# Hash-bucket attention and a max-out feed-forward on one core: operands transposed by DMA, exponentials as the stationary operand, feed-forward interleaved half-batch by half-batch

## The chip, the cores and the metric

One core of a Trainium2 chip. The metric is the device time of one execution in microseconds. Runs of one kernel on one chip differ by 0.3 to 5% here; a run more than 1.5% above the fastest of its kernel counts as slow, and verdicts use the others ("fast runs"). Engines: TensorE (PE; its weight loads, PEld, overlap its matmuls), VectorE (DVE), ScalarE (ACT), GpSimd (POOL), SyncE (SP), which issues DMAs.

## The reference

Attention over 4 batches x 8 heads x 768 tokens x 64 dimensions. A query sees only the keys whose 6-bit hash (signs of a projection) equals its own; a query without such a key gets the mean of v. The result, as 3072 tokens x 512, goes through a feed-forward with three input weights.

```python
q_bucket = sum(((q @ proj) > 0) * 2**arange(6)); k_bucket likewise
scores = where(q_bucket == k_bucket, 0.125 * q @ k.T, -1e9)
attn = softmax(scores) @ v                      # per head, 768 x 768
x = attn as (3072, 512)
h = max(x @ w1, x @ w2, x @ w3)                 # 512 -> 768
out = h @ w_out                                 # 768 -> 512
```

The six bits are appended to the 64 dimensions of q and k as large numbers, so one matmul with 70 rows gives score plus a bucket term, and Exp with a bias turns unequal buckets into zeros.

## The kernel before

A pair of heads at a time: fp32 q and k are transposed on TensorE, copied out of PSUM, hashed by fp32 matmuls; then scores, Exp in two pieces, and attention-value (AV) matmuls with v stationary and 768 exponentials moving. The denominators land on one row and go through DRAM to become a factor on all rows. After all 16 pairs comes the feed-forward.

```python
def prep(pi):                                    # [cut: loads]
    for natt, dsts in ((qnat, qa), (knat, ka)):
        mp = misc_ps.tile([P, S], FP32, tag="m1")
        for c in range(NCH):
            nc.tensor.transpose(mp[:, c*P:(c+1)*P], natt[:, c, :], iden[:])      # L107
        nc.vector.tensor_copy(dsts[0][0:D, :], mp[0:D, :])                       # L108
        nc.vector.tensor_copy(dsts[1][0:D, :], mp[D:2*D, :])
    # [cut] bps <- P2, qa / ka in fp32 (L114, L116); signs written into rows 64..69
def body(pi):
    for hd, von in ((0, voneA), (1, voneB)):
        for c in range(NCH):
            # [cut] two score matmuls, 512 + 256 columns (L147)
            nc.scalar.activation(AT[:, 0:512], sc[:, 0:512], ActFn.Exp, ...)     # L150
            nc.scalar.activation(AT[:, 512:768], sc[:, 512:768], ActFn.Exp, ...) # L151
            nc.tensor.matmul(av[0:65, 0:512], von[:, c, :], AT[:, 0:512], ...)   # L154
            nc.tensor.matmul(av[0:65, 512:768], von[:, c, :], AT[:, 512:768], ...)
        # [cut] svp <- v column sums (L158); row 64 through DRAM; normalise into xT
prep(0)
for pi in range(NPAIR):
    if pi + 1 < NPAIR: prep(pi + 1)
    body(pi)
# [cut] then the feed-forward over 6 chunks of 512 tokens (L221, L232)
```

The softmax here doesn't subtract the row's maximum and nothing guards it: scores larger than these inputs give would overflow.

Of the kernel before, what the change touches and what calls it, by code (L numbers as in the profile page):

```python
# [11 lines left out]
BF16 = mybir.dt.bfloat16  # L12
# [5 lines left out]
def kernel(  # L18
# [17 lines left out]
    NT = B * S  # L36
    DM = H * D
    DF = moe_w1.shape[1]
    NPAIR = (B * H) // 2
    HPAIR = H // 2  # L40
    NB2 = D + NBITS

    SCALE = 0.125
    EXP_BIAS = -SCALE * 256.0 * NBITS

    konst = ctx.enter_context(tc.tile_pool(name="konst", bufs=1))
    wpool = ctx.enter_context(tc.tile_pool(name="wpool", bufs=1))
    xpool = ctx.enter_context(tc.tile_pool(name="xpool", bufs=1))

    iden = konst.tile([P, P], FP32, name="iden")  # L50
    make_identity(nc, iden[:])
    P2 = konst.tile([P, NBITS], FP32, name="P2")
    nc.sync.dma_start(P2[0:D, :], proj[:, :])
    ones_row = konst.tile([P, D], FP16, name="ones_row")
    nc.vector.memset(ones_row[:], 1.0)
    bias_t = konst.tile([P, 1], FP32, name="bias_t")
    nc.vector.memset(bias_t[:], EXP_BIAS)

    w1_sb = wpool.tile([P, DM // P, DF], FP16, name="w1_sb")
    w2_sb = wpool.tile([P, DM // P, DF], FP16, name="w2_sb")  # L60
    w3_sb = wpool.tile([P, DM // P, DF], FP16, name="w3_sb")
    for w_sb, w_ap in ((w1_sb, moe_w1), (w2_sb, moe_w2), (w3_sb, moe_w3)):
        nc.gpsimd.dma_start(w_sb[:], w_ap.rearrange("(c p) f -> p c f", p=P))
    wout_sb = wpool.tile([P, DF // P, DM], FP16, name="wout_sb")
    nc.gpsimd.dma_start(wout_sb[:], moe_w_out.rearrange("(c p) m -> p c m", p=P))

    xT = [xpool.tile([P, NT], FP16, name=f"xT{j}", tag=f"xT{j}") for j in range(DM // P)]

    NVBUF = 3
    vone_tiles = [konst.tile([P, NCH, D + 1], FP16, name=f"vone{i}", tag=f"vone{i}")  # L70
                  for i in range(2 * NVBUF)]
    for t in vone_tiles:
        nc.vector.memset(t[:, :, D : D + 1], 1.0)

    att_ctx = ExitStack()
    nat = att_ctx.enter_context(tc.tile_pool(name="nat", bufs=4))
    ptile = att_ctx.enter_context(tc.tile_pool(name="ptile", bufs=3))
    atp = att_ctx.enter_context(tc.tile_pool(name="atp", bufs=10))
    small = att_ctx.enter_context(tc.tile_pool(name="small", bufs=4))
    drp = att_ctx.enter_context(tc.tile_pool(name="drp", bufs=4, space=bass.MemoryType.DRAM))  # L80
    sc_ps = att_ctx.enter_context(tc.tile_pool(name="sc_ps", bufs=2, space=bass.MemoryType.PSUM))
    misc_ps = att_ctx.enter_context(tc.tile_pool(name="misc_ps", bufs=1, space=bass.MemoryType.PSUM))
    av_ps = att_ctx.enter_context(tc.tile_pool(name="av_ps", bufs=1, space=bass.MemoryType.PSUM))

    pair_state = {}

    def prep(pi):
        b = pi // HPAIR
        jj = pi % HPAIR
        hA, hB = 2 * jj, 2 * jj + 1  # L90
        qnat = nat.tile([P, NCH, 2 * D], FP32, tag="qnat")
        knat = nat.tile([P, NCH, 2 * D], FP32, tag="knat")
        nc.sync.dma_start(qnat[:, :, 0:D], q[b, hA].rearrange("(c p) d -> p c d", p=P))
        nc.sync.dma_start(qnat[:, :, D : 2 * D], q[b, hB].rearrange("(c p) d -> p c d", p=P))
        nc.sync.dma_start(knat[:, :, 0:D], k[b, hA].rearrange("(c p) d -> p c d", p=P))
        nc.sync.dma_start(knat[:, :, D : 2 * D], k[b, hB].rearrange("(c p) d -> p c d", p=P))
        voneA = vone_tiles[(pi % NVBUF)]
        voneB = vone_tiles[NVBUF + (pi % NVBUF)]
        nc.gpsimd.dma_start(voneA[:, :, 0:D], v[b, hA].rearrange("(c p) d -> p c d", p=P))
        nc.gpsimd.dma_start(voneB[:, :, 0:D], v[b, hB].rearrange("(c p) d -> p c d", p=P))  # L100

        qa = [ptile.tile([NB2, S], FP32, tag="qaA", name="qaA"), ptile.tile([NB2, S], FP32, tag="qaB", name="qaB")]
        ka = [ptile.tile([NB2, S], FP32, tag="kaA", name="kaA"), ptile.tile([NB2, S], FP32, tag="kaB", name="kaB")]
        for natt, dsts in ((qnat, qa), (knat, ka)):
            mp = misc_ps.tile([P, S], FP32, tag="m1")
            for c in range(NCH):
                nc.tensor.transpose(mp[:, c * P : (c + 1) * P], natt[:, c, :], iden[:])  # L107
            nc.vector.tensor_copy(dsts[0][0:D, :], mp[0:D, :])  # L108
            nc.vector.tensor_copy(dsts[1][0:D, :], mp[D : 2 * D, :])

        for src, qside in ((qa, True), (ka, False)):
            bps = misc_ps.tile([P, S], FP32, tag="m1")
            for col0, nn in ((0, 512), (512, 256)):
                nc.tensor.matmul(bps[0:NBITS, col0 : col0 + nn], P2[0:D, :],  # L114
                                 src[0][0:D, col0 : col0 + nn], start=True, stop=True)
                nc.tensor.matmul(bps[64 : 64 + NBITS, col0 : col0 + nn], P2[0:D, :],  # L116
                                 src[1][0:D, col0 : col0 + nn], start=True, stop=True)
            for hd, base in ((0, 0), (1, 64)):
                o = src[hd][D : D + NBITS, 0:S]
                i_ = bps[base : base + NBITS, 0:S]  # L120
                if qside:
                    nc.vector.tensor_scalar(out=o, in0=i_, scalar1=0.0, scalar2=0.5,  # L122
                                            op0=AluOp.is_gt, op1=AluOp.subtract)
                else:
                    nc.vector.tensor_scalar(out=o, in0=i_, scalar1=0.0, scalar2=1024.0,  # L125
                                            op0=AluOp.is_gt, op1=AluOp.mult)
                    nc.vector.tensor_scalar(out=o, in0=o, scalar1=512.0, scalar2=None,
                                            op0=AluOp.subtract)
        pair_state[pi] = (qa, ka, voneA, voneB)

    def body(pi):
        b = pi // HPAIR
        jj = pi % HPAIR
        xt_tile = xT[jj]
        xcol = b * S
        qa, ka, voneA, voneB = pair_state.pop(pi)
        qab = [t.bitcast(BF16)[:, 1::2] for t in qa]
        kab = [t.bitcast(BF16)[:, 1::2] for t in ka]

        avs_h = []  # L140
        for hd, von in ((0, voneA), (1, voneB)):
            av = av_ps.tile([65, 1024], FP32, tag="av")
            for c in range(NCH):
                AT = atp.tile([P, S], FP16, tag="AT")
                sc = sc_ps.tile([P, S], FP32, tag="sc")
                for col0, nn in ((0, 512), (512, 256)):
                    nc.tensor.matmul(sc[:, col0 : col0 + nn],  # L147
                                     kab[hd][0:NB2, c * P : (c + 1) * P],
                                     qab[hd][0:NB2, col0 : col0 + nn], start=True, stop=True)
                nc.scalar.activation(AT[:, 0:512], sc[:, 0:512], ActFn.Exp, bias=bias_t[:], scale=SCALE)  # L150
                nc.scalar.activation(AT[:, 512:768], sc[:, 512:768], ActFn.Exp, bias=bias_t[:], scale=SCALE)  # L151
                st = c == 0
                sp = c == NCH - 1
                nc.tensor.matmul(av[0:65, 0:512], von[:, c, :], AT[:, 0:512], start=st, stop=sp)  # L154
                nc.tensor.matmul(av[0:65, 512:768], von[:, c, :], AT[:, 512:768], start=st, stop=sp)  # L155
            svp = sc_ps.tile([P, S], FP32, tag="sc")
            for c in range(NCH):
                nc.tensor.matmul(svp[0:D, 0:1], von[:, c, 0:D], ones_row[:, 0:1],  # L158
                                 start=(c == 0), stop=(c == NCH - 1))
            avs = small.tile([65, 776], FP32, tag="avs")  # L160
            nc.scalar.copy(avs[0:65, 0:768], av[0:65, 0:768])  # L161
            nc.vector.tensor_copy(avs[0:D, 768:769], svp[0:D, 0:1])  # L162
            avs_h.append(avs)

        for hd in (0, 1):
            avs = avs_h[hd]
            dlt = small.tile([65, S], FP16, tag="dlt")
            nc.vector.tensor_scalar(out=dlt[64:65, :], in0=avs[64:65, 0:768], scalar1=0.01,
                                    scalar2=None, op0=AluOp.is_lt)
            dra = drp.tile([S], FP32, tag="dra")  # L170
            drb_ = drp.tile([S], FP16, tag="drb_")
# [24 lines left out]
    for pi in range(NPAIR):  # L196
        if pi + 1 < NPAIR:
            prep(pi + 1)
        body(pi)
# [68 lines left out]
```

## Time and profile before

510.6 us, the median of 2 runs (506.13 and 515.07); the profiled run spans 517.3 us. By the rule above the slower of the two is a slow run, and so is the profiled one.

| stage of the span | us | what fills it |
|---|---|---|
| start | 0-25 | TensorE waits for q and k |
| attention | 25-386 | no engine full; TensorE at 0.68-0.83 of its clock |
| feed-forward | 386-517 | TensorE full, clock 1.0 |

The span in 40 slices of 12.9 us (kernel before), busy tenths, and the granted TensorE clock (the share of its full clock that TensorE was given) in tenths:

```profile
PE   0258888899879798989889788898989999999996
...
PEclk9999969757796877566676996757579999999999
```

The next lines are stretches of the same trace: busy time and count of each engine, then granted clock, DMA share and GB/s.

```profile
100.00:200.00 100.00, 85.75 (x398) 39.06 (x398) 67.83 (x110) 61.88 (x120) 37.91 (x65) 0.78 0.37 64
200.00:300.00 100.00, 88.63 (x376) 42.29 (x376) 64.19 (x104) 58.91 (x114) 35.29 (x62) 0.69 0.31 52
400.00:450.00 50.00, 49.02 (x228) 22.12 (x227) 20.12 (x29) 13.55 (x24) 0.25 (x1) 1.00 0.13 49
```

The attention stage has TensorE 86-89% busy at a reduced clock, DVE 64-68%, ACT about 60%: a chain rather than a full engine. The costliest groups there (the page's list: busy us and mean ns of one, then idle time before and what ended it):

```profile
L150 ACT ACTIVATE AT<-sc,bias_t 128x512 f16<-128x512 f32 x192 | 132.2, 689 | 140.5 <-PE sc L147 140.4
L151 ACT ACTIVATE AT<-sc,bias_t 128x256 f16<-128x256 f32 x192 | 90.9, 473 | 0.0
...
L114 PE MATMUL bps<-kaA,P_69 64*6 64x512 f32 (+1 forms) x64 | 35.2, 692 | 11.3 <-DVE qaB L122 11.3
L107 PE MATMUL mp<-iden,qnat 128*128 128x128 f32 x96 | 30.2, 394 | 16.7 <-DMA qnat<-in_q_dram 14.1
```

One line of the timeline (start, length, engine, line): six matmuls of one column, each with its own 64-column weight load. One takes 0.171 us, so (0.35 - 0.17) / 5 = 36 ns from start to start.

```profile
65.45 0.35 PE L158 MATMUL svp<-ones_row,vone_88 128*64 128x1 f16 x6
```

### The profile page before, as it was taken

How to read it: one execution, taken by the hardware profiler on the slowest of the kernel's cores; microseconds unless marked ns; L12 is line 12 of the kernel's file. 1: busy time of each engine (PE TensorE's matmuls, PEld its weight loads, DVE VectorE, ACT ScalarE, POOL GpSimd, SP SyncE). 2: the span in 40 equal slices, each digit the busy share in tenths (PEclk: the TensorE clock that was granted, in tenths of full speed). 3: DMA queues.
4: the chain of work that ended last, by engine and by line, in shares of the span. 5: the costliest groups of instructions: out<-in, count | busy, mean ns of one | idle time of the engine just before them, and what ended most of it. 6: DMA issues, size and time to landing. Idle time of an engine off the chain costs nothing.

```text
span 517.3 us, 5907 instructions
## 1 busy us (share of the span) xinstructions
PE 440.8 (85%) x1984; PEld 205.4 (40%) x1984; DVE 287.6 (56%) x464; ACT 253.4 (49%) x477; POOL 133.0 (26%) x234
## 2 busy tenths in 40 slices
PE   0258888899879798989889788898989999999996
PEld 0113433425334253534444344443444444444442
DVE  0145658756776667565575785766437353353442
ACT  0005857648575565555655676556682313323232
POOL 6000434423433334333333443323233000000000
PEclk9999969757796877566676996757579999999999
DMA  9994524415242533414141321201010202102012
GB/s 155 186 213 100 90 36 86 83 26 93 40 85 39 86 55 63 85 25 86 24 84 25 40 33 24 25 16 24 10 32 18 89 0 82 62 20 82 22 61 83
DMA packets 88367, 32.16 MB, mean 62 GB/s; under 512 B 80912, under 2 KB 84240, under 8 KB 88336
## 3 DMA queue, kind: packets, MB, share of 16 engines
q0 software_dynamic: 34624, 12.89, 17.7%
q1 hardware_dynamic: 53712, 18.88, 14.8%
q8 instruction: 16, 0.26, 0.2%
q14 instruction: 15, 0.12, 0.1%
HBM read 31.56 MB, written 6.49 MB: 74 GB/s over the span
## 4 chain that ended last, share of the span: by engine, by line
PE 58%; issue 12%; DVE 11%; DMA 9%; ACT 6%; POOL 3%; ACTq 0%; POOLq 0%; DVEq 0%
PE av L154 10%; PE sc L147 9%; PE bps L114 8%; PE pso L232 6%; PE mp L107 5%; ACT AT L150 5%; PE av L155 5%; DMA vone_87<-in_v_dram 4%; DVE avs L189 2%; DVE qaB L122 2%; DVE qaA L122 1%; ACT avs L161 1%; DMA dra<-avs 1%; PE svp L158 1%; DMA drb__335<-r_339 1%
## 5 line engine op out<-in xcount | busy, mean ns | idle before, releaser
L150 ACT ACTIVATE AT<-sc,bias_t 128x512 f16<-128x512 f32 x192 | 132.2, 689 | 140.5 <-PE sc L147 140.4
L151 ACT ACTIVATE AT<-sc,bias_t 128x256 f16<-128x256 f32 x192 | 90.9, 473 | 0.0
L147 PE MATMUL sc<-qaB,kaB 70*128 70x512 bf16 x192 | 67.8, 461 | 0.0
L221 PEld LDWEIGHTS <-w_sb 128*128 128x128 f16 x432 | 42.3, 98 | 51.0 <-issue 0.3
L147 PE MATMUL sc<-qaA,kaA 70*128 70x512 bf16 x192 | 55.0, 389 | 0.5 <-DVE avs L162 0.5
L114 PE MATMUL bps<-kaA,P_69 64*6 64x512 f32 (+1 forms) x64 | 35.2, 692 | 11.3 <-DVE qaB L122 11.3
L107 PE MATMUL mp<-iden,qnat 128*128 128x128 f32 x96 | 30.2, 394 | 16.7 <-DMA qnat<-in_q_dram 14.1
L161 ACT COPY avs<-av 65x768 f32<-65x768 f32 x32 | 25.4, 795 | 28.9 <-PE av L155 28.9
L116 PE MATMUL bps<-kaB,P_69 64*6 64x512 f32 (+1 forms) x64 | 35.4, 695 | 0.0
L147 PEld LDWEIGHTS <-kaB 70*128 70x128 bf16 x192 | 25.0, 131 | 25.0 <-issue 19.0
L189 DVE SCALAR_TENSOR_TENSOR avs<-dltb,avs 64x768 f32<-64x768 f16 x32 | 31.9, 997 | 0.4
L125 DVE TENSOR_SCALAR kaA<-bps 6x768 f32<-6x768 f32 x16 | 15.2, 949 | 26.8 <-PE bps L116 26.8
L147 PEld LDWEIGHTS <-kaA 70*128 70x128 bf16 x192 | 22.1, 115 | 19.6 <-issue 12.7
L108 DVE COPY qaA<-mp 64x768 f32<-64x768 f32 x16 | 15.1, 946 | 25.5 <-PE mp L107 25.5
L108 DVE COPY kaA<-mp 64x768 f32<-64x768 f32 x16 | 15.2, 950 | 25.0 <-PE mp L107 24.9
L107 PEld LDWEIGHTS mp<-iden,qnat 128*128 128x128 f32 x96 | 18.0, 204 | 27.5 <-issue 23.5
L114 PE MATMUL bps<-qaA,P_69 64*6 64x512 f32 (+1 forms) x64 | 25.2, 517 | 3.6 <-issue 2.1
L235 ACT COPY osb<-pso 128x512 f32<-128x512 f32 x24 | 14.1, 586 | 28.8 <-PE pso L232 28.8
L107 PE MATMUL mp<-iden,knat 128*128 128x128 f32 x96 | 18.8, 342 | 9.2 <-DMA knat<-in_k_dram 8.4
L116 PE MATMUL bps<-qaB,P_69 64*6 64x512 f32 (+1 forms) x64 | 25.2, 517 | 0.0
L122 DVE TENSOR_SCALAR qaA<-bps 6x768 f32<-6x768 f32 x16 | 15.2, 949 | 16.4 <-PE bps L116 16.3
L154 PE MATMUL av<-AT,vone_87 128*65 128x512 f16 x36 | 16.9, 468 | 7.7 <-ACT AT L150 7.0
(882 smaller groups left out, 841.4 us busy)
## 6 DMA issues: line engine op xcount, KB each, us to landing
qnat<-in_q_dram SPq DMA_DIRECT2D x32, 192.0 KB, 3.0
knat<-in_k_dram SPq DMA_DIRECT2D x32, 192.0 KB, 3.2
out_dram<-osb SPq DMA_DIRECT2D x24, 256.0 KB, 2.0
dltb<-ddl POOLq DMA_DIRECT2D x32, 96.0 KB, 2.6
w_sb<-in_moe_w_dram POOLq DMA_DIRECT2D x3, 768.0 KB, 11.3
wout_sb<-in_moe_w_out_dram POOLq DMA_DIRECT2D x1, 768.0 KB, 19.2
vone_87<-in_v_dram POOLq DMA_DIRECT2D x6, 96.0 KB, 3.2
vone_90<-in_v_dram POOLq DMA_DIRECT2D x6, 96.0 KB, 3.2
```

Source lines behind the costliest of these rows:

```text
L107: nc.tensor.transpose(mp[:, c * P : (c + 1) * P], natt[:, c, :], iden[:])
L114: nc.tensor.matmul(bps[0:NBITS, col0 : col0 + nn], P2[0:D, :], src[0][0:D, col0 : col0 + nn], start=True, stop=True)
L116: nc.tensor.matmul(bps[64 : 64 + NBITS, col0 : col0 + nn], P2[0:D, :], src[1][0:D, col0 : col0 + nn], start=True, stop=True)
L122: nc.vector.tensor_scalar(out=o, in0=i_, scalar1=0.0, scalar2=0.5, op0=AluOp.is_gt, op1=AluOp.subtract)
L147: nc.tensor.matmul(sc[:, col0 : col0 + nn], kab[hd][0:NB2, c * P : (c + 1) * P], qab[hd][0:NB2, col0 : col0 + nn], start=True, stop=True)
L150: nc.scalar.activation(AT[:, 0:512], sc[:, 0:512], ActFn.Exp, bias=bias_t[:], scale=SCALE)
L151: nc.scalar.activation(AT[:, 512:768], sc[:, 512:768], ActFn.Exp, bias=bias_t[:], scale=SCALE)
L154: nc.tensor.matmul(av[0:65, 0:512], von[:, c, :], AT[:, 0:512], start=st, stop=sp)
L161: nc.scalar.copy(avs[0:65, 0:768], av[0:65, 0:768])
L189: nc.vector.scalar_tensor_tensor(out=avs[0:D, 0:768], in0=dltb[:, :], scalar=avs[0:D, 768:769], in1=avs[0:D, 0:768], op0=AluOp.mult, op1=A ...
L221: nc.tensor.matmul(psx[:, :], w_sb[:, jc, fb * P : (fb + 1) * P], xT[jc][:, tcx * TOK : (tcx + 1) * TOK], start=(jc == 0), stop=(jc == NJC ...
L232: nc.tensor.matmul(pso[:, :], hts[fb][:, tb * P : (tb + 1) * P], wout_sb[:, fb, :], start=(fb == 0), stop=(fb == NFB - 1))
```

## The change

Intent: take the fp32 work and the PSUM copies off the attention stage, halve the AV columns, drop the DRAM round trips, and let the feed-forward fill TensorE while attention waits.

- q and k are **split** on DVE into an fp16 pair (value and remainder), side by side in 128 columns, and **transposed by DMA** (40 transposes of 384 KB). Hashes are fp16 matmuls on the pair, four column groups at once.
- **AV is turned round**: a 128x128 block of exponentials is stationary, 65 columns of v and ones move. The denominator is then a column, and normalising stays on the chip (DVE; POOL adds the mean of v where it is needed).
- The order is fixed by hand. A **step** is one score/Exp/AV unit (two key chunks, half the queries of one head); there are 192. A **half-batch** is 24 steps. When one is complete it is transposed by DMA into xT, and its 21 feed-forward groups are dealt out over later steps by a **credit** counter.

```diff
-            nc.tensor.transpose(mp[:, c * P : (c + 1) * P], natt[:, c, :], iden[:])
+            nc.vector.tensor_scalar(out=s[:, :, 0:D], in0=x32, scalar1=QS, ...)          # L121
+            nc.vector.scalar_tensor_tensor(out=s[:, :, D : 2 * D], in0=x32, scalar=QS,
+                                           in1=s[:, :, 0:D], ...)                        # L122
+            nc.sync.dma_start_transpose(t[:], s[:].rearrange("p a d -> p (a d)"))        # L125
 [cut: hashes, L133; score, L186, and one Exp of 768 columns, L190]
-            nc.tensor.matmul(av[0:65, 0:512], von[:, c, :], AT[:, 0:512], ...)
+                nc.tensor.matmul(av[:, o : o + D + 1], AT[:, i, c * P : (c + 1) * P],    # L206
+                                 vones[b % 2][:, 2 * pr + hh, 2 * j + i, 0 : D + 1], ...)
 [cut: norm: dd, rr, xn on DVE; m, t and an add on POOL; DMA transpose xT<-xn, L233]
+    def prep_at(b, pr, s):
+        at(s, lambda: split(b, pr))
+        at(s + 6, lambda: hash_a(b, pr))
+        at(s + 7, lambda: hash_b(b, pr))
 [cut: the step of every load, split and hash]
+    first = NUG + 8                      # NUG = 24 steps a half-batch
+    rate = total / (N - first + 2)
+    for u in range(N + LAG):
+        score(u); attend(u - LAG); the step's preparation   # shortened
+        if u >= first and u < N:
+            credit += rate
+            while atoms and credit >= atoms[0][0] / 2:
+                cost, fn = atoms.pop(0)
+                credit -= cost
+                fn()
+    for _, fn in atoms: fn()
```

## The prediction

> **What bounds it now.** The busy table by stretch shows three stages. Start: about 25 us of waiting for loads (14.1 us for q, 8.4 for k in the list of groups). Attention: to about 386 us; TensorE busy 86-89%, but at a granted clock of only 0.68-0.83, and no engine is full (DVE 64-68%, ACT about 60%): a pair's chain of waits, with TensorE most of it (58% of the whole chain). Feed-forward: the last 131 us, TensorE full at clock 1.0; 128x512 matmuls start 216 ns apart in the timeline.
>
> **Removed** (group list): fp32 transposes on TensorE (49 us busy) with their PSUM copies (61 us of DVE); fp32 hash matmuls (121 us busy, two side by side, so about 60); the reciprocal's DRAM round trips (160 DMAs of 2.1-2.7 us, mostly hidden, plus 62 us of DVE); 192 of 384 Exp calls (689+473 ns become one of 768 columns; the slope of 0.84 ns/column gives about 905: 223 -> 174 us of ACT).
> **Added**: DVE splits (16 x 2 x 1.55 us = 50 us), 40 DMA transposes of 384 KB, POOL casts and mean-value fix, 1152 attention matmuls of 65 columns with exponentials stationary instead of 384 of 512+256.
> **Moved**: feed-forward interleaved with attention; same 295k columns, about 124 us.
>
> **Sum for TensorE, warm**: feed-forward 124, scores 62, attention-value 1152 x about 60 ns = 69 (an estimate: 64-column weight loads of svp started 32-36 ns apart in the timeline, so 128 columns about 55-60), hashes 10 (four column groups side by side, as the two of L114/L116 start within 10 ns), mean values 5: about 270 us. ACT about 202, DVE about 190. TensorE stays the limit: a unit of attention with its feed-forward share takes about 1.5 us there, 1.07 on ACT.
>
> **What keeps it above 270.**
> 1. Start: load, split, transpose, hash: about 20 us. The Trainium skill ("Advanced Engine Details and Errata", X-Bar Transpose) says transposing DMAs run as fast as plain ones; from the 3 us loads here I take 4-5 us each. No run shows it yet.
> 2. The first 32 units have no feed-forward, four pairs' transposes to wait for, and a half clock: about 55 us.
> 3. The pacing spends credit faster than half-batches arrive. In the instruction order, at steps 73, 97, 121, 145, 169 the first feed-forward matmuls (2, 6, 11, 15, 19 groups at once) come right after the last attention matmul of their own half-batch, so in-order TensorE stands through normalisation, POOL add and transposing DMA: about 8 us each, and the clock falls (the skill's "TensorE: Matmul & The Clock Gate", Part 1: half rate after about 3.4 us idle): 45-50 us in all. Bursts on two PSUM buffers: 5-10 us.
> 4. Tail: the last half-batch's chain (8 us), its feed-forward alone (18), store (2).
>
> 20 + 55 + 230 (160 units at 0.77 plus 107) + 15 + 48 + 28 = 396; parts overlap, and the weight-load guess may be high: I predict 375 us, range 325 to 425. Faster by over 2%: 0.97; within 2%: 0.02; slower: 0.01.
>
> **Right or wrong will show in**: five TensorE gaps of 6-10 us, released by the transposing DMA into xT; ACT around 55% busy; the spacing of av matmuls; landing times of transposes; clock above 0.9 between gaps; a tail of about 28 us after the last Exp.
>
> **What would make it wrong**: transposes of 8 us or more each (40 x 8 = 320 us then bind); av matmuls at 100 ns (+46 us) or 35 ns (-29 us); the clock staying near half, as in attention now; DVE and POOL delaying each other.

## The result, and the profile after

429.31 us, the median of 2 runs (428.58 and 430.04): 0.846 of before (95% interval 0.839 to 0.852). Faster, as forecast, but 4 us outside the stated range. A ratio here is the mean time of one kernel's fast runs over that of the other's of the same rounds, so it is not quite the ratio of the medians. (The two times of each kernel do not give 0.846 exactly: with the fast run of before alone it would be 0.848.)

The page's slices of the changed kernel (10.7 us each):

```profile
PE   0406785887979916886589915979649983998396
...
PEclk9999658596999976989979965998758997999689
DMA  7996957973030493473110594147510101010201
```

PE now has dips to 0, 1 and 3 (waits at the start, then the stands: stretches in which TensorE does nothing because the next matmul in its order waits), and the clock still falls in many slices. Its groups, as above:

```profile
L190 ACT ACTIVATE AT<-sc,bias_t 128x768 f16<-128x768 f32 x192 | 165.2, 908 | 117.6 <-PE sc L186 116.6
L246 PE MATMUL ps<-xT,w_sb 128*128 128x384 f16 x576 | 125.4, 361 | 54.9 <-DMA xT<-xn 52.9
...
L133 PE MATMUL hps<-qT,PA 128*32 128x384 f16 x64 | 16.5, 400 | 47.9 <-DMA qT<-qs 35.2
```

The two idle columns are the news: TensorE stood 52.9 us for xT and 35.2 us for transposed q. Who waited for whom (total us, times, longest):

```profile
PE ps L246 <- DMA xT<-xn: 52.9, 7, 13.7
...
PE hps L133 <- DMA qT<-qs: 35.2, 6, 13.2
...
PE hps L133 <- DVE hb L144: 12.8, 6, 2.9
```

Four stretches of its trace: the start and the long wait at step 2, the rest of the first 32 steps, the interleaved part, the last feed-forward:

```profile
0.00:38.00 38.00, 8.75 (x64) 4.26 (x65) 13.10 (x31) 5.22 (x6) 7.73 (x13) 1.00 0.96 228
38.00:81.60 43.60, 30.60 (x293) 18.03 (x292) 26.09 (x51) 22.68 (x28) 18.60 (x25) 0.70 0.79 165
81.60:404.50 322.90, 242.51 (x2165) 142.19 (x2165) 150.09 (x299) 158.88 (x210) 87.14 (x121) 0.86 0.35 86
404.50:428.20 23.70, 19.68 (x90) 9.51 (x89) 8.03 (x14) 3.45 (x7) 0.00 (x0) 0.86 0.09 34
```

Two things read from the timeline. First, the AV matmuls: six in 0.35 us with one taking 0.19, so (0.35 - 0.19) / 5 = 32 ns each at full clock, where 60 was predicted.

```profile
118.74 0.35 PE L206 MATMUL av<-vone,AT 128*128 128x65 f16 x6
```

Second, one stand at xT, at step 73. The last AV matmul of the half-batch starts at 151.51; the next one is the first feed-forward matmul of the same half-batch, at 164.10:

```profile
149.60 3.57 SPq L125 DMA_TRANSPOSE qT<-qs  x1
...
151.51 0.35 PE L206 MATMUL av<-vone,AT 128*128 128x65 f16 x6
151.97 0.17 DVE L221 TENSOR_SCALAR dd<-av 128x6 f32<-128x6 f32 x1
...
153.27 3.89 SPq L125 DMA_TRANSPOSE kT<-ks  x1
153.44 0.91 POOL L230 TENSOR_TENSOR xn<-xn,t 128x384 f16<-128x384 f16 x1
...
157.89 2.02 SPq L233 DMA_TRANSPOSE xT<-xn  x1
164.10 0.48 PE L246 MATMUL ps<-xT,w_sb 128*128 128x384 f16 x1 [12.24 <-DMA xT<-xn]
```

Normalising is over at 154.35, but SP is still issuing the next batch's kT; xT is issued at 157.89 and lands 6.2 us later, where a lone xT lands in 3.65 us.

Where the 428.2 us went, against the sum in the prediction. "Work" is each matmul at its full-clock start-to-start spacing in this trace (384 columns 162.5 ns, 512 columns 216, AV 32, four hashes together 162); in the 24 us from 126 to 150 us these spacings add up to 24.1 us, so nothing is to spare. The step boundaries are the score matmuls.

| term | predicted | measured |
|---|---|---|
| to the first score | 20 | 16.6 |
| steps 0 to 31 | 55 | 65.0 (16.6 to 81.6) |
| TensorE work, steps 32 to 191 | 230 | 199.3 |
| stands at xT before the tail (predicted with their clock loss) | 48 | 46.7 |
| everything else in steps 32 to 191 | 15 | 70.7 (316.7 - 199.3 - 46.7) |
| tail (from 398.3) | 28 | 29.9 |
| sum | 396 | 428.2 |

The 70.7 us divide, by the start-to-start excess of each matmul, into about 24 in stretches at half clock, 21 in small delays of under 0.3 us (PSUM buffers in bursts, Exp), 18 in hash waits, 4 in other waits, and 4 for the mean-value matmuls, which the row of work leaves out. The division between clock and small delays is an attribution, not a measurement.

### The profile page after: what moved, and what is told of

Read it like the earlier page. It is cut to its first block, busy times and chain, and to the rows that moved or that the text cites. A ratio compares the mean times of both kernels' runs of the same rounds, so it can differ in the third digit from the quotient of the medians.

```text
span 428.2 us, 6629 instructions
## 1 busy us (share of the span) xinstructions
PE 301.5 (70%) x2608; PEld 174.0 (41%) x2608; DVE 197.3 (46%) x394; ACT 190.2 (44%) x249; POOL 113.5 (26%) x159
## 4 chain that ended last, share of the span: by engine, by line
PE 47%; DMA 21%; DVE 13%; ACT 8%; issue 4%; POOL 3%; SPq 2%; POOLq 0%; ACTq 0%; DVEq 0%
PE ps L246 24%; DMA kT<-ks 11%; PE sc L186 9%; DMA xT<-xn 8%; ACT AT L190 8%; PE po L258 6%; PE av L206 4%; PE hps L133 3%; DVE qs L122 3%; SPq L125 2%; DVE qs L121 2%; DVE ks L121 2%; DVE ht L253 1%; DMA v<-in_v_dram 1%; POOL xn L230 1%
## 5 line engine op out<-in xcount | busy, mean ns | idle before, releaser
L190 ACT ACTIVATE AT<-sc,bias_t 128x768 f16<-128x768 f32 x192 | 165.2, 908 | 117.6 <-PE sc L186 116.6
L246 PE MATMUL ps<-xT,w_sb 128*128 128x384 f16 x576 | 125.4, 361 | 54.9 <-DMA xT<-xn 52.9
L186 PE MATMUL sc<-qT,kT 70*128 70x384 f16 x384 | 104.7, 358 | 9.4 <-ACT AT L190 2.3
L253 DVE TENSOR_TENSOR ht<-ht,ps 128x384 f16<-128x384 f16 x96 | 53.1, 553 | 117.0 <-PE ps L246 114.1
L206 PEld LDWEIGHTS <-AT 128*128 128x128 f16 x1152 | 66.7, 103 | 32.4 <-issue 10.3
L206 PE MATMUL av<-vone,AT 128*128 128x65 f16 x1152 | 72.1, 201 | 0.6 <-ACT AT L190 0.4
L186 PEld LDWEIGHTS <-kT 70*128 70x128 f16 x384 | 36.3, 103 | 37.6 <-issue 22.3
L133 PE MATMUL hps<-qT,PA 128*32 128x384 f16 x64 | 16.5, 400 | 47.9 <-DMA qT<-qs 35.2
L258 PE MATMUL po<-wout_sb,ht 128*128 128x512 f16 x144 | 35.6, 385 | 0.5 <-DVE ht L253 0.4
L230 POOL TENSOR_TENSOR xn<-xn,t 128x384 f16<-128x384 f16 x32 | 30.5, 952 | 2.5
L225 POOL TENSOR_TENSOR t<-m,mv 128x384 f32<-128x384 f32 x32 | 26.5, 828 | 2.7
L144 DVE TENSOR_SCALAR hb<-hps 128x384 f16<-128x384 f32 x16 | 8.8, 551 | 29.9 <-PE hps L133 29.9
L159 POOL CAST vone<-v 128x768 f16<-128x768 f32 x16 | 17.7, 1104 | 16.7 <-DMA v<-in_v_dram 16.5
```

Source lines behind the costliest of these rows:

```text
L133: nc.tensor.matmul(hps[32 * g : 32 * (g + 1), 0:HQ], w[:], T[n, b, pr][:, hh * NCH + c0 : hh * NCH + c0 + CH, :], start=s, stop=not s)
L159: nc.gpsimd.tensor_copy(vones[b % 2][:, 2 * pr : 2 * pr + 2, :, 0:D], v32)
L186: nc.tensor.matmul(sc[:, i, 0:HQ], kT[0:KR, hh * NCH + 2 * j + i, :], qT[0:KR, hh * NCH + hf * CH : hh * NCH + (hf + 1) * CH, :], start=Tr ...
L190: nc.scalar.activation(AT[:], sc[:, :, 0:HQ], ActFn.Exp, bias=bias_t[:], scale=EXP_SCALE)
L206: nc.tensor.matmul(av[:, o : o + D + 1], AT[:, i, c * P : (c + 1) * P], vones[b % 2][:, 2 * pr + hh, 2 * j + i, 0 : D + 1], start=first, s ...
L225: nc.gpsimd.tensor_tensor(out=t[:], in0=m[:].to_broadcast([P, 2, CH, D]), in1=mvs[b, pr][:].unsqueeze(2).to_broadcast([P, 2, CH, D]), op=A ...
```

## The experiments

Two theories. **A**: the banked credit makes TensorE stand at xT, and those stands also bring the clock down. **B**: the loss sits in the hash waits, the late transposes and a half clock that comes with this mix of matmuls. "Fast mean" below is the mean of a run's fast times; the changed kernel has 429.3.

### e1: pacing

```diff
-    first = NUG + 8
-    rate = total / (N - first + 2)
+    rate = total / (2 * B) / NUG
+    DELAY = 5        # steps between a half-batch's xT transpose and its first group
-        if u >= first and u < N:
+        if u < N and atoms and atoms[0][2] <= u:     # no credit is banked
```

> Only the pacing of the feed-forward groups changes: each half-batch's groups become eligible 5 steps after its transposing DMA is issued, at one half-batch per 24 steps, and credit is not banked. Theory A (the banked credit makes TensorE stand at xT, and the half clock follows those gaps): the seven waits of TensorE for xT (52.9 us now) fall to one of about 6 us at the end, the clock after 120 us is above 0.93, and the time falls from 429 to about 370 (355 to 385). Rival B (the loss sits in the hash waits, late transposes and a half clock that this mix of matmuls brings with it): the waits for qT and hb grow in place of those for xT and the time stays above 405.

365.7 us median (fast mean 366.2), ratio 0.722 (0.714 to 0.730). Its slices:

```profile
PE   0221777737759999985889999855889999999895
...
PEclk9999966967889999997989999986989999999999
```

From the tenth slice on none is below 5 (the changed kernel has a 1 twice and a 3 twice there). Before the tail one wait for xT of more than 1 us is left (4.0 us), the mean clock rose from 0.86 to 0.92, and the time recorded at half clock fell from 122 to 58 us. After 120 us the clock is 0.95 (0.87 in the changed kernel). Theory A holds: the old pacing cost 63 us, of which 46 were waits for xT themselves (52.9 us fell to 6.6, the tail included). The edit changes the rate, the readiness of a half-batch and the banking together; their shares were not separated. And B is not empty: 16 us of hash waits remain after step 32, and two waits of 3.7 and 4.2 us for ht, a feed-forward result on DVE.

### e2: weights later

```diff
-    at(0, lambda: load_w(0)); at(1, lambda: load_w(1)); at(3, lambda: load_w(2))
+    at(15, lambda: load_w(0)); at(18, lambda: load_w(1)); at(21, lambda: load_w(2))
-    at(8, ... wout_sb ...)
+    at(24, ... wout_sb ...)
```

> Only the three expert weight loads move, from steps 0, 1, 3 to 15, 18, 21, and the output weight load from step 8 to 24 (first use is step 32). Theory: the transposing DMAs of the first pairs land late (up to 20 us against 3.2 us at best) because the casting weight loads share the DMA engines with them; then the 13.2 us wait for qT at step 2 falls to 3 to 6 us and the time falls by 8 to 14 us. Rival: the transposes are late because of the q, k, v loads or of themselves: the wait stays above 10 us and the time changes by under 4 us.

434.3 us (ratio 0.856, 0.845 to 0.867). The wait at step 2 fell from 13.2 to 6.1 us as the theory said, but a wait of 14.2 us appeared at step 28 (3.9 in the changed kernel), where the weights now met batch 1's transposes. The mechanism was right and the forecast of time wrong: the wait moved.

### e3: no interleaving

```diff
-        if u >= first and u < N:
+        if False:                       # all feed-forward groups after step 191
```

> No interleaving: all feed-forward groups come after the last attention unit (the eight xT tiles are kept; to make room, operand tiles go from 8 to 6 buffers and hidden tiles from 12 to 9). If the interleaving as paced now hides the feed-forward as intended, the time rises to 450 or more. If its stalls eat what it hides, as theory A says: attention alone at about 0.95 us a unit ends near 250 to 270 us, the feed-forward takes 126 to 136 us, together 385 to 405 us, below 429.

417.6 us (fast mean 415.9; ratio 0.820, 0.806 to 0.834), slightly above the expected range and below the changed kernel. So as it was paced, the interleaving lost about 13 us (by fast runs) against no interleaving at all; the whole gain over before came from the rewritten attention. Attention ended at 268.8 us here (386 before), and the feed-forward took 138 us.

### e4: hashes two steps later

```diff
-        at(s + 6, lambda: hash_a(b, pr)); at(s + 7, lambda: hash_b(b, pr))
+        at(s + 8, lambda: hash_a(b, pr)); at(s + 9, lambda: hash_b(b, pr))
```

> For batches 1 to 3 the two hash steps of a pair move from 6 and 7 to 8 and 9 steps after its split, so that the next pair's split (5 steps after) is through on DVE before the hash results are read. Theory: the six waits of the hash matmuls for hb (12.8 us) come from the split standing ahead of the PSUM read in DVE's order, and part of the waits for qT from too short a lead; both shrink by two thirds and the time falls by 8 to 16 us. Rival: they are slack of the xT stalls, and the time changes by under 4 us.

428.3 us, ratio 0.848 (0.833 to 0.862): no change. The waits of the hash matmuls for hb vanished, but waits of 1.1 to 3.0 us for ht (the feed-forward's maximum on DVE) took their place: the split stands ahead of whatever comes next in DVE's queue. The rival fits the time; the theory fits the mechanism.

### e5, e6, e7, e8: batch preparation, weights, split

```diff
 e8, on the changed kernel; e5, on e1:
-        s0 = (2 * b - 1) * NUG
+        s0 = (2 * b - 1) * NUG + 8
 e6 = e5 with load_w at 6, 11, 15 and wout at 19
 e7 = e6 with split(b, pr, "q") at s and split(b, pr, "k") at s + 2
```

> The changed kernel with its own pacing, and only the preparation of batches 1 to 3 moved 8 steps later. Theory: the two long stands at xT (12.2 and 13.7 us) are long because the next pair's transposes stand ahead of xT in the SP queue and loads share the engines; both fall to about 6.2 us as the others, and the first 32 steps get 5 us shorter: 429 falls to 408 to 418. Rival: the length of those stands is the norm chain of DVE and POOL: they stay above 10 us, time above 422.

e8: 413.2 us (fast mean 412.3), ratio 0.809 (0.803 to 0.814). The time was as expected, the reason only in part: step 32 was reached at 76.5 us in place of 81.6 and hash waits after it fell from 18 to 5 us, but the stands at xT at steps 73, 97 and 121 were 10.2, 8.8 and 9.2 us in its profile (a slow run; 12.2, 6.2 and 13.7 before). That the loads now fall on the half-batch boundary may be why; it was not tested.

> The pacing of e1, and everything that prepares batches 1 to 3 (loads, splits, transposes, hashes) 8 steps later. Theory: the first 80 us are held by what the DMA engines are asked for, and batch 1's loads and transposes are asked for 24 steps early; later, its transposes no longer stand ahead of xT in the SP queue. The step-28 wait for qT (4.8 + 2.6 us in e1) vanishes, step 32 is reached 5 to 9 us earlier, time 352 to 361 against 366. Rival: the waits move with the work and the time stays within 3 us of e1.

e5: 355.1 us (fast mean 354.9), ratio 0.696 (0.692 to 0.700): 11 us below e1, within the expectation. Step 32 was reached at 82.3 us against 86.1 in e1 (less than expected), and hash waits after it fell from 16 to 6 us, while those for the feed-forward's operands and buffers (before the tail) grew from 15 to 22, and a wait of 5.3 us for the first xT appeared before step 32.

> e5 with the weight loads spread over steps 6, 11, 15 and 19 in place of 0, 1, 3 and 8. Theory: with batch 1 out of the way there is room for the weights later, so the 13 us wait at step 2 falls to about 6 us without a new one (in e2 it came back at step 28): time 344 to 356, 5 to 10 us below e5. Rival: total DMA demand before the first feed-forward decides, so the wait comes back at the first feed-forward group and the time equals e5 within 3 us.

e6: 354.9 us in one submission and 354.0 in another (runs from 347 to 359, fast mean 350.4 in the first). Against e5 unclear. The waits at step 2 fell to 2.0 + 3.2 us, but the wait at the first xT grew from 5.3 to 10.5 us: the rival.

> e6 with the k half of each split of batches 1 to 3 two steps after the q half. Theory: the split holds DVE for about 4.6 us at a stretch (measured 1.1 + 1.3 us per tensor, 1.55 was predicted) and so holds PSUM buffers of hash and feed-forward groups; halved, the waits of TensorE for hb and ht (2.9 to 4.2 us each in e1) fall below 1 us each: 5 to 10 us below e6. Rival: DVE has slack enough, same as e6 within 3 us.

e7: 374.2 us, 19 us slower than e6 (by fast runs 371.3 against 350.4). A failed idea: the later k half made its transpose late (a 6.9 us wait for kT) and gave two blocks on DVE in place of one.

### e9: half of the split on ACT

```diff
-            nc.vector.tensor_scalar(out=s[:, :, 0:D], in0=x32, scalar1=QS, scalar2=None, op0=AluOp.mult)
+            nc.scalar.activation(s[:, :, 0:D], x32, ActFn.Copy, scale=QS)
```

> e6 once more, unchanged, because its four runs lay between 348 and 359 us; beside e9 on one chip. 348 to 360 us.

> e6 with the first operation of each split (scale and round to fp16) on ACT in place of DVE. ACT is about half busy, so its 0.9 us twice a pair should cost nothing. Theory: feed-forward and hash results wait in DVE's order behind a split of about 4.6 us and hold the two PSUM buffers, which makes the TensorE waits for ht of 2.2 to 2.9 us; with half the split gone from DVE those waits fall below 1.5 us each and the time falls by 5 to 12 us below e6. Rival: the splits on ACT delay the Exp that TensorE waits for, and the time stays within 3 us or grows, as in e7.

346.9 us (fast mean 345.7) beside 354.0 for e6 on the same chip, whose only fast run was 347.3. By medians 7 us better, by fast runs 2: unclear. The waits for ht fell from 2.9 to about 2.0 us, not below 1.5.

### e10: does the clock follow gaps, or thin work?

```diff
 on e3:
+            fp = mm_ps.tile([P, 512], FP32, tag="mm", name="fp")
+            for _ in range(2):
+                nc.tensor.matmul(fp[:, 0:HQ], ones[:], fill[:], start=True, stop=True)
```

> e3 (feed-forward after attention) with two idle matmuls of 128x128 by 384 columns in every step, into a PSUM buffer that nobody reads: 0.325 us more TensorE work a step, 62 us in all, on constant data. In e3 TensorE ran 98 percent busy at a granted clock of 0.51 from 100 to 134 us with no gap above 1.3 us. Theory C: the half clock comes from too little work per time in this mix, not from gaps alone; then the fill lifts the clock of the attention stage above 0.9 and the time stays within 10 us of e3 (417) in spite of 62 us more work. Rival: the half clock follows the waits for the transposing DMAs; the clock stays near 0.6 there and the time grows by 30 us or more.

421.0 us beside 417.6 for e3 (fast means 421.0 and 415.9; ratios 0.835 and 0.820 to before, intervals overlapping): 62 us more TensorE work for about 5 us. Two stretches of e3, then about the same two of e10:

```profile
100.00:134.00 34.00, 33.30 (x278) 21.17 (x278) 12.04 (x26) 28.61 (x32) 17.22 (x24) 0.51 0.30 76
80.00:269.00 189.00, 155.64 (x1536) 94.69 (x1535) 94.96 (x198) 135.74 (x161) 85.67 (x118) 0.73 0.53 115
```

```profile
100.00:134.00 34.00, 33.94 (x399) 21.70 (x393) 15.02 (x36) 30.06 (x36) 15.66 (x24) 0.95 0.33 84
80.00:280.00 200.00, 173.47 (x1905) 105.75 (x1905) 98.58 (x207) 139.14 (x164) 85.56 (x120) 0.91 0.53 116
```

In e3 TensorE is 98% busy for 34 us and yet at half clock; with the fill the clock is 0.95. Busy is not the same as much work: at the full-clock spacings given above, the matmuls of this stretch are 17.6 us of work in e3 and 31.9 us in e10. So the clock is not set by gaps alone: score and AV matmuls without feed-forward beside them can stay at half rate. The fill differs from the real work in shape (128 rows against 70) and in data (constants), so which property counts is open.

### e11: first feed-forward later

```diff
 on e9:
-    rate = total / (2 * B) / NUG
+    rate = total / (2 * B) / (NUG - 2)
-        ready = (2 * b + hf + 1) * NUG + 1 + DELAY
+        ready = (2 * b + hf + 1) * NUG + 1 + (DELAY if b or hf else 12)
```

> e9 with the first half-batch's feed-forward eligible 12 steps after its transposing DMA is issued in place of 5, and one half-batch per 22 steps in place of 24 so that the later ones catch up. Theory: the 10 us stand at the first xT in e9 is DMA demand (weights, batch 1, transposes) that is only late, not too much; seven more attention steps fit into it. The stand falls below 3 us, time 337 to 343 against 347. Rival: the attention steps moved forward are bound by ACT and meet batch 1's transposes earlier, time within 3 us of e9.

351.6 us, ratio 0.687 (0.667 to 0.706): no gain. In its profile (a slow run) step 32 came at 68.9 us, but 8.2 us of waiting for qT came back for batch 1. The rival.

### e12 and e13: one load taken away

```diff
 e12, on the changed kernel (wrong result on purpose):
-        nc.gpsimd.dma_start(w_sb[i][:], w_ap.rearrange("(c p) f -> p c f", p=P))
+        nc.vector.memset(w_sb[i][:], 0.01)
 e13, on the changed kernel: without nc.gpsimd.tensor_scalar(out=m...), tensor_tensor(out=t...), tensor_tensor(out=xv...)
```

> The changed kernel with the three expert weight loads taken away (constants are written in their place; a wrong result on purpose). Theory: the first 32 steps took 65 us where 55 were predicted because the DMA engines are asked for too much at once: without 4.7 MB of weight reads the 13 us wait for qT at step 2 falls to 6 us or less without a new wait, step 32 is reached at 66 us or before in place of 81.6, and the time falls to 412 to 418. Rival: the transposes are slow of themselves, step 32 is reached after 75 us and the time stays above 423.

e12: 429.3 us (fast mean 425.8), ratio 0.840 (0.828 to 0.851): no clear change. In its profile (a slow run) the wait at step 2 fell to 5.8 us, but pair 3's hash at step 13 then waited 5.5 + 3.3 us, and step 32 was reached at 79.4. Two stretches of it, to be held against the first two of the changed kernel above (DMA share 0.96 and 0.79):

```profile
0.00:38.00 38.00, 13.54 (x104) 7.39 (x104) 24.23 (x42) 8.38 (x9) 5.90 (x12) 1.00 0.86 187
38.00:82.00 44.00, 27.74 (x275) 16.17 (x269) 24.58 (x48) 20.97 (x25) 20.47 (x28) 0.78 0.72 155
```

So e12 gives no sign that the weights' share of the DMA demand sets the first 80 us; the rest of the demand was not tested, as the DMA engines stayed busy. Nor was it a clean removal: the output weight was still loaded at step 8, and the three memsets took 2.62 us each on DVE, one of which held up a hash by 2.3 us at step 7.

> The changed kernel without the three POOL operations a head pair that put in the mean value for queries with no key in their bucket (wrong for such queries on purpose). It shortens the chain before each xT transpose by about 1.5 us, and takes 64 us of work from POOL, which shares time with DVE in the traces (the first split operation took 0.55 us at best but 0.71 in the middle and 1.2 at worst). Theory: seven stands at xT get 1 to 1.5 us shorter and the splits shorter: 412 to 422 us. Rival: POOL's share does not matter, above 425.

e13: 443.9 us, 15 us slower with less work. The stands that nothing disturbs did fall from 6.2 to 4.3 us (the two long ones rose, to 16.5 and 14.5), but POOL, which also issues the loads, issued batch 1's first load at 30.9 us in place of 55.5, among batch 0's transposes; hash waits before step 32 rose from 28 to 41 us, and steps 0 to 31 took 78 us in place of 65. (The first score also came 4 us later; why was not followed up.) Both theory and rival missed this.

### e14 and e15: more lead

```diff
 e14 on e9, e15 on e11:
-    at(2, lambda: split(0, 2)); at(7, lambda: split(0, 3))
+    at(0, lambda: split(0, 2)); at(4, lambda: split(0, 3))      # batch 0 all on DVE
-        at(s + 6, lambda: hash_a(b, pr)); at(s + 7, lambda: hash_b(b, pr))
+        at(s + 8, lambda: hash_a(b, pr)); at(s + 9, lambda: hash_b(b, pr))
```

> e9 with longer leads: the splits of pairs 2 and 3 of batch 0 move from steps 2 and 7 to 0 and 4 (on DVE), and the hashes of batches 1 to 3 from 6 and 7 to 8 and 9 steps after their split. Theory: the first 32 steps are long because a pair's split and two transposes need 8 us or more and the schedule gives them 5 or 6 steps of about 1 us, whatever the DMA load (e12 took 13 us of DMA work away and gained nothing): hash waits before step 32 fall from 13 to under 6 us and those after it from 4 to under 2, time 336 to 342. Rival: the waits move to the next transposes or to DVE, within 4 us of e9 (347).

> The same longer leads on e11 (first half-batch's feed-forward 12 steps late). Theory: e11 gained nothing because batch 1's hash then came too early for its transposes (8.2 us); with two more steps of lead that wait falls below 3 us, time 334 to 341. Rival: DMA demand moves the wait on again, within 4 us of e11 (352).

e14: **330.1 us** (328.5 to 336.5), ratio 0.647 (0.638 to 0.655), 23% below the changed kernel and the best version; its result is correct. e15: 339.8 us, ratio 0.666: also better than its base, but ACT, which does half of the splits, stood 3.3 us for a load of q at 58 us, and a score behind it waited 5.4 us. e14's slices:

```profile
PE   0233997088889999787898999687889999899795
...
PEclk9999999679999999989999999899999999999998
```

No hash wait above 0.3 us is left after step 32, those before it fell from 12.5 to 10.4 us (more than the 6 expected), time at half clock fell from 41 us in e9 to 21 (mean clock 0.971), and waits for ht fell to 1.7 us. One stand of 10.7 us at the first xT is left: that xT was issued at 55.18 us and took 11.7 us to land, with the DMA engines full (share 1.10 from 55 to 67 us, 1.01 from 17.6 to 56.2). So with longer leads e14 is 16 us faster by fast runs, and DMA volume may well be what limits its start (not tested). It changes three things at once (the lead of two splits, that of the hashes, and batch 0's scaling back on DVE), so it does not say which of them gave more; the hash lead alone had gained nothing in e4.

| run | median us | ratio to before |
|---|---|---|
| changed kernel | 429.3 | 0.846 |
| e3 no interleaving | 417.6 | 0.820 |
| e8 preparation 8 steps later | 413.2 | 0.809 |
| e1 pacing | 365.7 | 0.722 |
| e5 pacing and preparation | 355.1 | 0.696 |
| e9 also weights spread, half split on ACT | 346.9 | 0.685 |
| e14 also longer leads | 330.1 | 0.647 |

## Why the prediction was right or wrong

**Right: direction and limit.** TensorE stayed the busiest engine (301.5 us) and the largest part of the chain that ended last (47%), the fp32 work went, and Exp took 908 ns at 768 columns (905 predicted). Of the other signs that were named, the clock between the stands was 0.91 after step 32 (above 0.9 predicted), the tail 29.9 us (28) and ACT 44% busy (55%).

**Right: the stands.** "in-order TensorE stands through normalisation, POOL add and transposing DMA: about 8 us each": measured 12.2, 6.2, 13.7, 6.2 and 6.2 us at the five steps named, plus 2.2 us at step 52; 46.7 us. The mechanism was right; that the total meets the 48 is partly luck, because the 48 were to hold the clock's loss too, and that came on top. e1 removed nearly all of them and gained 63 us, against 50 to 60 us predicted for stands, clock and bursts together.

**Wrong in size, to the good: AV.** "1152 x about 60 ns = 69": measured 32 ns, 37 us. The estimate scaled 64-column weight loads by length. The Trainium skill ("TensorE: Matmul & The Clock Gate", Weight-path perf modes) says that loads of exactly 128 weights use a faster path unless their type is fp32; the 32 ns spacing agrees with that, but no run here switched the path off. The spacings of this trace give an estimate of what is left: (216 - 162.5) / 128 = 0.42 ns per moving column, so 65 moving columns alone come to about 29 ns, and the weight load seems to be hidden. I had read that section and not applied it; the prediction did name 35 ns among what would make it wrong.

**Wrong: the step that failed is the 15 us in "20 + 55 + 230 (160 units at 0.77 plus 107) + 15 + 48 + 28 = 396"**, together with the 21 us that were then taken off. The deduction was earned (work came out 31 us lower), but everything else in the interleaved part took 70.7 us. What it consists of, and what showed it:
- Half clock outside the stands. The sum had room for the clock only in the 48 us, which the stands alone used up; about 24 us were lost outside them in the interleaved part. e3 shows that the clock can stay at half while TensorE is 98% busy, when attention matmuls run alone, and e10 that more matmuls lift it. That the same happens after each stand of the changed kernel is inferred: all eleven half-clock stretches that begin after 43 us, but for the one at the very end, begin during a wait of TensorE of over 1.6 us, or within 2 us of its end; but two such waits (2.2 us at 123 us, 2.9 us at 194 us) brought none.
- Waits for hashes and for DVE. I had none after step 32; 18 us were hash waits. The split took longer than the 1.55 us per tensor in the prediction: its two operations took 0.55 and 0.96 us at best, but 1.2 and 1.56 at worst, and 2.0 together on average. The timeline of the changed kernel, just before the stand shown above, has a scaling of 1.22 us that begins 0.04 us after POOL began a cast of 0.83 us (lines below). The Trainium skill ("SBUF — State Buffer", Who interferes with whom) says that a DVE instruction of this kind can contend with POOL for a pair of ports that they share, and that the later one then waits for the other's whole instruction; 1.22 us beside the cast against 0.55 at best agrees, but no run took the cast away. e4, e7 and e9 show that moving the split about trades one wait for another; the hash waits after step 32 fell to 5 us when the preparation came later (e8), and went when e14 added lead to that.

**Wrong by 10 us: the first 32 steps.** "Four pairs' transposes to wait for" was right, and "4-5 us each" was not: qT landed 3.2 us after issue at best, 6.3 in the middle, 19.8 at worst. My first explanation, contention with the weight loads, found no support in e12: taking them away gained nothing clear. What fits is that the schedule gives a pair's split and transposes five or six steps, which last only about 1 us each when there is no feed-forward between them; e14 gave them more and brought step 32 forward (70.2 us after 77.3 in e9), though only 2 us of that are hash waits; e9 also spent 6.8 us at half clock before its first xT, e14 none. Contention is the other half: e13 brought loads into that time and lost 13 us there.

```profile
149.15 0.83 POOL L159 CAST vone<-v 128x768 f16<-128x768 f32 x1
149.19 1.22 DVE L121 TENSOR_SCALAR ks<-k 128x768 f16<-128x768 f32 x1
```

What stays open: whether less DMA traffic would shorten the first xT of e14, and what the clock counts as work.

## What to carry to other kernels

When work is dealt out by a credit counter, credit must not be banked while there is nothing to spend it on: it comes back as a burst at the worst moment, on an in-order engine that then stands for its own inputs. A hand-made schedule should count leads in time, not in steps: where steps get shorter, the same number of steps is less lead, and here taking the weights' traffic away did not make up for it. Check a new interleaving against the same kernel without it; here that one run (e3) showed at once that the gain came from elsewhere.

## What the Trainium skill lacked or had wrong

- "TensorE: Matmul & The Clock Gate", Part 1, ties half rate to idle windows of about 3.4 us, and in one more case to frequent short idles between groups of matmuls. It gives no measure of how much work counts as busy. In e3 TensorE was 33.30 of 34 us busy, without a gap after 100.7 us, at a clock of 0.51; adding 62 us of fill in e10 raised the same stretch to 0.95.
- The same page, Back-to-back issue gap, gives about 81 ns per load-and-matmul pair at 128 columns (131 ns at 512) and nothing for fewer; with 65 columns and 128x128 fp16 weights the pairs here started 32 ns apart, and with 512 columns 216 ns apart.
- "Advanced Engine Details and Errata", X-Bar Transpose (TRN2), says transposing DMAs are as fast as regular ones. Alone that is so: xT of 384 KB landed in 3.65 us, a q load of the same size in 3.9 in the middle and 3.15 at best. Beside loads qT took 6.3 us in the middle and 19.8 at worst, of which the page says nothing.
- No page has a measured time for how long issuing a transposing DMA holds the issuing queue on this chip: SP was held 1.3 us at best and 9.0 at worst per transpose of 384 KB, so that an urgent xT waited behind q and k.
